# A spectral mixer on one Trainium2 core: a fixed instruction order in the front, paired evacuations, and half of the later filter loads issued from GpSimd

## The chip, the cores and the metric

The kernel runs on one core of one Trainium2 chip. The metric is the device time of one execution in microseconds (us), and smaller is better. The core has five engines that run side by side: TensorE (matmuls), VectorE, ScalarE, GpSimd, and SyncE, which here does nothing but issue transfers. In profile lines they are PE, DVE, ACT, POOL and SP, and a trailing q (as in SPq) marks the sequencer that issues a transfer. Sixteen DMA engines move the data between memory and the core.

Every number below is of fast runs of one core, unless the text says otherwise. A profile is one of the executions. Its span, from the first to the last traced instruction, is 1.5 to 2.1 us shorter than the time of the same execution.

## The reference, cut to what matters

```python
def _A_ref(x, w_r, w_i):                 # x: 1 x 2048 x 512, w: 2048 x 257, all bf16
    X = rfft2(x.astype(float32), axes=(-2, -1))
    X = X * (w_r + 1j * w_i)             # the "filter" W
    return irfft2(X, s=(2048, 512), axes=(-2, -1)).astype(bfloat16)

x  = A_x
h  = x + _A_ref(layernorm(x), A_w_r, A_w_i)
h2 = h + _B_ref(layernorm(h), B_w1, B_b1, B_w2, B_b2)   # token MLP with GELU: not touched here
```

The Fourier transforms are done as matrix products. The change touches only the start, up to the product with the filter.

## The kernel before

The program makes a list of operations and a scheduler orders them on each engine. The operations that matter here come in this order.

1. X comes in as 16 tiles of 128x512, and a constant matrix FP in four pieces. Per tile, the statistics of the layer norm are taken, ScalarE makes the reciprocal deviation `rs`, and FS = FP * rs is made on one of three engines.
2. The first transform (f1) multiplies FS with X. ScalarE copies the result out of PSUM to Y, in halves of 512 columns:

```python
for q in range(8):
    for b in range(2):
        unit = PsumUnit("f1", 1)
        ...                                   # 8 matmuls for tiles 2q and 2q+1
        if (q, b) in Y_DVE:                   # three of the sixteen
            dve(f"y_{q}_{b}", lambda eng, bank, ...: eng.tensor_copy(dst, src(bank)), ...)
        else:
            act(f"y_{q}_{b}", dst, src, ACT.Copy, 512, unit=unit, prio=28)
```

3. The second transform (f2) needs all tiles of Y. Behind it VectorE multiplies with the filter, eight products V, of which the first and the last are cut in halves, so ten operations:

```python
def tt(eng, bank, ...):
    return eng.tensor_tensor(vout, s, win, ALU.mult)       # V = ps * W
K.op(f"v_{u}_{h}", "dve", tt, ins=[wt], outs=[vout], ..., after=wload[u])
```

The filter is read in 28 pieces, in three groups, for products 0, 1 to 3, and 4 to 7. A product waits for all pieces of its group:

```python
for ch, (u0, u1) in enumerate(((0, 1), (1, 4), (4, 8))):
    g0, ng = 4 * u0, 4 * (u1 - u0)
    lst = []
    for w, dram in ((0, A_w_r), (1, A_w_i)):               # real, imaginary
        for comp in range(2):
            d = W[comp::4, g0:g0 + ng, w, :]
            lst.append(dma(f"ld_wp{ch}_{w}{comp}", d,
                bass.AP(dram.tensor, g0 * LW, [[64 * LW, 32], [LW, ng], [1, LW]]),   # rows of 514 bytes
                32 * ng * 514, prio=42 - ch, group=f"w{ch}", rate=300.0))
            ...                                            # the mirrored piece, and two rows for group 0
    for u in range(u0, u1):
        wload[u] = lst
```

Before these pieces SyncE issues X in six pieces, two pieces of FP and the matrices E and MR. The other two pieces of FP are issued by ScalarE.

Of the kernel before, what the change touches and what calls it, by code (L numbers as in the profile page):

```python
# [6 lines left out]
ACT = mybir.ActivationFunctionType  # L7
ALU = mybir.AluOpType
LN_EPS = 1e-5
# [81 lines left out]
def build_consts():  # L91
    c = {}
    n1 = np.arange(NP)
    fp = np.zeros((NP, NS2, NG, 2, 2), np.float64)
    inv = np.zeros((NP, NS2, NP), np.float64)
    for n2 in range(NS2):
        sidx = 16 * n1 + n2
        for g in range(NG):
            gp = _gpos(g)
            for s in range(2):  # L100
                k1 = _slot_k1(g, s)
                c0 = g * 4 + s
                if k1 == 0:
                    fp[:, n2, gp, 0, s] = 1.0
                    fp[:, n2, gp, 1, s] = (-1.0) ** n1
                    inv[c0, n2, :] = 1.0 / S_LEN
                    inv[c0 + 2, n2, :] = ((-1.0) ** n1) / S_LEN
                else:
                    a = TWO_PI * ((k1 * sidx) % S_LEN) / S_LEN
                    fp[:, n2, gp, 0, s] = np.cos(a)  # L110
                    fp[:, n2, gp, 1, s] = -np.sin(a)
                    inv[c0, n2, :] = 2.0 * np.cos(a) / S_LEN
                    inv[c0 + 2, n2, :] = -2.0 * np.sin(a) / S_LEN
    fp = fp.reshape(NP, NS2, NP)
    fp = np.stack([-fp, fp], axis=2)
    for q in range(4):
        c[f"FP{q}"] = fp[:, 4 * q:4 * q + 4]
    c["IF"] = inv
    e = np.zeros((NP, 2, 2, 2, NP), np.float64)
    d2 = np.zeros((NP, 2, 2, 256), np.float64)  # L120
    j = np.arange(NP)
    for par in range(2):
        l = 2 * j + 1 + par
        for dblk in range(2):
            d = dblk * NP + np.arange(NP)
            a = TWO_PI * ((d[:, None] * l[None, :]) % D_LEN) / D_LEN
            e[:, dblk, par, 0, :] = np.cos(a)
            e[:, dblk, par, 1, :] = -np.sin(a)
        d = np.arange(256)
        a = TWO_PI * ((l[:, None] * d[None, :]) % D_LEN) / D_LEN  # L130
        d2[:, par, 0, :] = np.cos(a) / D_LEN
        d2[:, par, 1, :] = np.sin(a) / D_LEN
    e[:, :, 1, 1, 127] = 0.0
    d2[127, 1, 0, :] *= 0.5
    d2[127, 1, 1, :] = 0.0
    m = np.zeros((NP, 2, 2, NP), np.float64)
    for i in range(2):
        mm = _fwd_matrices(i == 1)
        m[0:64, i] = mm
        m[64:128, i] = mm  # L140
    r = np.stack([_inv_matrices(False), _inv_matrices(True)], axis=1)
    c["E"] = e.reshape(NP, 1024)
    c["MR"] = np.concatenate([m.reshape(NP, 512), r.reshape(NP, 512)], axis=1)
    c["D2"] = d2.reshape(NP, 1024)
    return c
# [33 lines left out]
class Builder:  # L179
    def __init__(self, nc, limits):  # L180
        self.nc = nc
        self.ops = []
        self.writer = {}
        self.readers = {}
        self.tensors = {}
        self.limits = limits
        self.cell_cache = {}

# [37 lines left out]
    def op(self, name, engine, emit, ins=(), outs=(), occ=100.0, lat=None, unit=None, pr=False, pw=False,  # L226
           first=False, last=False, prio=0, nbytes=0, is_dma=False, not_before=0.0, after=(), group=None, rate=DMA_RATE):
# [13 lines left out]
        o.rate = rate  # L241
        deps = {id(d): d for d in after}
# [38 lines left out]
    def schedule(self):  # L281
# [13 lines left out]
        order = []  # L295
        while len(order) < len(ops):
            best = None
            for o in ready:
                bank, avail = None, 0.0
# [22 lines left out]
            ready.remove(o)  # L322
            o.sched, o.start = True, st
# [11 lines left out]
            if o.is_dma:  # L335
                x0 = max(st + (3200.0 if st < 4000.0 else 1700.0), dma_free)
                dma_free = x0 + o.bytes / o.rate
                o.finish = dma_free + 200.0
            else:
                o.finish = st + o.lat  # L340
# [143 lines left out]
STAT_ACT = (1, 3)  # L484
RS_GROUPS = ((0,), (2,), (4,), (5,), (6, 7), (8, 9), (10, 11), (12,), (13,), (14,), (15,))
FS_ENG = {4: "act", 7: "act", 9: "dve", 11: "dve", 13: "dve", 14: "act", 15: "dve"}
Y_DVE = ((5, 1), (6, 1), (7, 1))
# [7 lines left out]
def build_kernel(nc, A_x, A_w_r, A_w_i, B_w1, B_b1, B_w2, B_b2, out):  # L495
# [5 lines left out]
    K = Builder(nc, {"f1": 6, "f2": 2, "x": 2, "g1": 2, "g2": 2, "g3": 2, "mm1": 5, "mm1b": 6, "mm2": 8})  # L501
# [13 lines left out]
    def dma(name, dst, src, nbytes, stream="sp", outs=(), ins=(), prio=0, strided=False, after=(), group=None, rate=DMA_RATE,  # L515
            not_before=0.0):
        def emit(eng, bank):
            if strided:
                with nc.allow_non_contiguous_dma(reason="small bias gather"):
# [3 lines left out]
                    rate=rate, occ=1000.0 if stream == "pool" else 640.0 if rate < DMA_RATE else 460.0, not_before=not_before)  # L523
# [40 lines left out]
    def ldf(q, pr_, stream="sp", nb=0.0):  # L564
        sl = slice(4 * q, 4 * q + 4)
        dma(f"ld_FP{q}", FP[:, sl, :, :], cin[f"FP{q}"][:, :, :, :], 1 << 18, outs=[FP[:, sl, :, :]], prio=pr_, stream=stream, not_before=nb)

    for q, (a, b) in enumerate(((0, 2), (2, 4), (4, 6), (6, 8), (8, 12))):
        ldx(a, b, 90 - q)
    ldf(2, 84)  # L570
    ldx(12, 16, 83)
    ldf(3, 82)
    ldf(0, 90, "act")
    act("table", T["tb"][:, 0:1], EPS[:, 0:1], ACT.Abs_reciprocal_sqrt, 1, ins=[EPS[:, 0:1]], prio=88)
    ldf(1, 87, "act", 1800.0)
# [3 lines left out]
    for ch, (u0, u1) in enumerate(((0, 1), (1, 4), (4, 8))):  # L579
        g0, ng = 4 * u0, 4 * (u1 - u0)  # L580
        lst = []
        for w, dram in ((0, A_w_r), (1, A_w_i)):
            for comp in range(2):
                d = W[comp::4, g0:g0 + ng, w, :]
                lst.append(dma(f"ld_wp{ch}_{w}{comp}", d, bass.AP(dram.tensor, g0 * LW, [[64 * LW, 32], [LW, ng], [1, LW]]),
                               32 * ng * 514, prio=42 - ch, group=f"w{ch}", rate=300.0))
# [3 lines left out]
                               32 * nh * 514, prio=42 - ch, group=f"w{ch}", rate=300.0))  # L590
                if g0 == 0:
                    d = W[2 + comp::4, 0, w, :]
                    lst.append(dma(f"ld_wz{ch}_{w}{comp}", d, bass.AP(dram.tensor, 32 * LW, [[64 * LW, 32], [1, LW]]),
                                   32 * 514, prio=42 - ch, group=f"w{ch}", rate=300.0))
# [21 lines left out]
    ZT, BV = T["ZT"], T["bv"]  # L616
    K.op("zt", "dve", lambda eng, bank: eng.memset(ZT[:, :], 0.0), outs=[ZT[:, :]], occ=200.0, prio=60)  # L617
# [9 lines left out]
    def fs_op(i):  # L627
        e = FS_ENG.get(i, "pool")
        rs = RS[:, i:i + 1]
        if e == "act":  # L630
            act(f"fs{i}", FS[:, i, :, :], FP[:, i, :, :], ACT.Copy, 256, ins=[FP[:, i, :, :]], scale=rs, prio=30)
        else:
            dve(f"fs{i}", lambda eng, bank: eng.tensor_scalar(FS[:, i, :, :], FP[:, i, :, :], rs, None, op0=ALU.mult),  # L633
                [FP[:, i, :, :], rs], [FS[:, i, :, :]], 120, prio=30, engine=e, lat=920.0 if e == "pool" else None)

    def stat_act(i):
# [3 lines left out]
        nm = NM[:, i:i + 1]  # L640
        dve(f"nm_{i}", lambda eng, bank: eng.tensor_scalar(nm, SM[:, i:i + 1], -1.0 / D_LEN, None, op0=ALU.mult), [SM[:, i:i + 1]], [nm], 1, prio=33, engine="pool", lat=210.0)
        dve(f"bv_{i}", lambda eng, bank: eng.tensor_scalar(BV[:, i:i + 1], nm, nm, LN_EPS, op0=ALU.mult, op1=ALU.subtract), [nm], [BV[:, i:i + 1]], 1, prio=33, engine="pool", lat=210.0)
        act(f"rs_{i}", RS[:, i:i + 1], V1[:, i:i + 1], ACT.Abs_reciprocal_sqrt, 1, ins=[V1[:, i:i + 1]], bias=BV[:, i:i + 1],
            scale=-1.0 / D_LEN, prio=32)
        fs_op(i)

    def stat_dve(grp):
        a, b = grp[0], grp[-1] + 1
        for i in grp:
# [3 lines left out]
            dve(f"st_{i}", lambda eng, bank, i=i, x=x: eng.bn_stats(ST[:, i, 0:6], x), [x], [ST[:, i, 0:6]], 512, prio=25)  # L653
# [15 lines left out]
    Yv = Y[:].rearrange("p b y g (n k) -> p b (y g) n k", k=4)  # L669
    for q in range(8):  # L670
        for b in range(2):
            unit = PsumUnit("f1", 1)
            lastmm = {}
            for n in range(2):
                n2 = 2 * q + n
                lo = X[:, n2, b * NP:b * NP + NP]
                hi = X[:, n2, 256 + b * NP:256 + b * NP + NP]
                f = FS[:, n2, 1, :]
                f2 = bass.AP(f.tensor, f.offset, [list(f.ap[0]), [0, 2], [1, NP]])
                fm = FS[:, n2, :, :]  # L680

                def o(bank, n=n):
                    return ps[:, bank, n * 256:n * 256 + 256]
                mm(f"f1_{n2}_{b}a", o, lo, f2, unit, True, False, n == 0, 14, 256, ins=[lo, f])
                lastmm[n] = mm(f"f1_{n2}_{b}b", o, hi, fm, unit, False, True, False, 14, 256)

            def src(bank):
                v = ps[:, bank, :].rearrange("p (n g k) -> p n g k", n=2, k=4)
                return v.rearrange("p n g k -> p g n k")
            dst = Yv[:, b, :, 2 * q:2 * q + 2, :]  # L690
            if (q, b) in Y_DVE:
                dve(f"y_{q}_{b}", lambda eng, bank, dst=dst, src=src: eng.tensor_copy(dst, src(bank)), [], [dst], 512, unit=unit, prio=28)
            else:
                act(f"y_{q}_{b}", dst, src, ACT.Copy, 512, unit=unit, prio=28)
            for n in range(2):
                for w_ in range(WARM_AFTER[2 * q + n] if b == 1 else 0):
                    warm(f"warmf{q}{n}{w_}", wu, 13, after=[lastmm[n]], last=2 * q + n == LAST_WARM)
# [183 lines left out]
```

## Time and profile before

| | before |
|---|---|
| time, median of the first 3 runs (lowest to highest) | 134.06 us (133.94 to 134.62) |
| span of the profile, mean granted TensorE clock | 132.4 us, 1.000 |
| front, to the end of ScalarE's last Y (VectorE's last ends at 18.93) | 18.57 us |
| first V operation starts; last one ends | 21.48; 39.36 us |
| filter group 1 / 2 / 3 complete in the trace | 15.37 / 22.90 / 30.11 us |

The first view is part 4 of the page of before, the chain of work that ended last, by engine and line with its share of the span. TensorE holds half of it, and the V products are the next largest entry.

```profile
PE ps L531 50%; DVE V L739 13%; DVE H L799 7%; ACT Y L549 5%; DVE TT L790 4%; DVE TT L792 4%; DVE HH L804 4%; DMA X<-in_A_x_dram 3%; POOL FS L633 1%; ACT rs L549 1%; ACT FS L549 1%; ACT JK L549 1%; DVE OUT L829 1%; ACT PQ L549 0%; PE ps L62
```

The next is the timeline of VectorE in before: start, duration, engine, source line, operation, output and inputs, count, and in brackets how long the engine was idle just before and what ended that idleness. The ten V operations run in one block from 21.48 us without a wait worth showing. After them VectorE waits for TensorE, and from 42.63 us it is the busy engine.

```profile
21.48 17.88 DVE L739 TENSOR_TENSOR V<-ps,W 128x1024 bf16<-128x1024 f32 x10 [0.94 <-PE ps L531]
42.63 0.42 DVE L790 TENSOR_TENSOR TT<-ps,X 128x256 f32<-128x256 f32 x1 [3.27 <-PE ps L531]
```

The timeline of SyncE's sequencer in before shows when the filter pieces are issued: group 1 from 5.80 us (twelve pieces), group 2 from 13.66 us, group 3 from 18.97 us (eight pieces each). Each issue takes about 0.65 us.

```profile
5.80 3.95 SPq L521 DMA_DIRECT2D W<-in_A_w_r_dram  x6
...
13.66 2.60 SPq L521 DMA_DIRECT2D W<-in_A_w_r_dram  x4
16.30 2.62 SPq L521 DMA_DIRECT2D W<-in_A_w_i_dram  x4
18.97 3.33 SPq L521 DMA_DIRECT2D W<-in_A_w_r_dram  x4
```

The last line comes from the timeline of ScalarE in before. Two 512-column evacuations take 1.06 us from the first's start to the second's end; one starts every 0.48 us.

```profile
9.93 1.06 ACT L549 ACTIVATE Y<-ps 128x512 bf16<-128x512 f32 x2
```

### The profile page before, as it was taken

The page shows a single profiled execution, that of the slowest core. Times are in us where ns is not written, and L with a number is a line of the kernel's source. Part 1 is how long each engine was busy: PE and PEld are TensorE (multiplying, and loading weights), DVE is VectorE, ACT ScalarE, POOL GpSimd, SP SyncE. Part 2 cuts the span into 40 slices and gives each one's busy share as a digit, 9 for nine tenths or more (in the row PEclk, how much of TensorE's full clock was granted, in tenths as well). Part 3 has the DMA queues.
Part 4 walks back from the last instruction along what each step waited for, and adds up shares of the span by engine and source line. Part 5 has one row for each costly group of instructions (what it writes and reads, how often), then busy time and mean ns, then how long its engine had stood idle before and what let it go on. Part 6 is the DMA issues. An engine that isn't in the chain of part 4 may idle for free.

```text
span 132.4 us, 2013 instructions
## 1 busy us (share of the span) xinstructions
PE 123.7 (93%) x776; PEld 74.5 (56%) x786; DVE 69.3 (52%) x127; ACT 63.3 (48%) x146; POOL 12.4 (9%) x33
## 2 busy tenths in 40 slices
PE   6989989999977979999999999999999999999990
PEld 2436656788666736544434444456666666666660
DVE  0499867999981999999960000000242332423322
ACT  4579976978966999986689322222000000000000
POOL 0199920000300000000000000000000000000000
PEclk9999999999999999999999999999999999999999
DMA  2999699999999999992000000000111112111121
GB/s 80 375 396 364 153 244 273 286 322 283 419 426 417 410 408 411 417 295 74 0 0 0 0 0 0 5 0 0 40 40 70 49 40 82 42 57 62 40 79 40
DMA packets 16648, 22.16 MB, mean 167 GB/s; under 512 B 2720, under 2 KB 12960, under 8 KB 16128
## 3 DMA queue, kind: packets, MB, share of 16 engines
q1 hardware_dynamic: 16352, 21.52, 47.5%
q10 hardware_dynamic: 288, 0.52, 1.1%
q8 instruction: 6, 0.10, 0.3%
q14 instruction: 2, 0.02, 0.0%
HBM read 19.95 MB, written 2.10 MB: 167 GB/s over the span
## 4 chain that ended last, share of the span: by engine, by line
PE 51%; DVE 32%; ACT 9%; DMA 3%; POOL 2%; issue 1%; DVEq 0%; ACTq 0%
PE ps L531 50%; DVE V L739 13%; DVE H L799 7%; ACT Y L549 5%; DVE TT L790 4%; DVE TT L792 4%; DVE HH L804 4%; DMA X<-in_A_x_dram 3%; POOL FS L633 1%; ACT rs L549 1%; ACT FS L549 1%; ACT JK L549 1%; DVE OUT L829 1%; ACT PQ L549 0%; PE ps L621 0%
## 5 line engine op out<-in xcount | busy, mean ns | idle before, releaser
L531 PE MATMUL ps<-HH,W 128*128 128x512 bf16 (+1 forms) x173 | 40.3, 379 | 1.3 <-DVE HH L804 0.9
L531 PE MATMUL ps<-GT,W 128*128 128x512 bf16 (+1 forms) x172 | 37.9, 379 | 0.2
L829 DVE SCALAR_TENSOR_TENSOR OUT<-ps,B2f,H 128x512 bf16<-128x512 f32 x16 | 12.0, 750 | 48.7 <-PE ps L531 48.7
L531 PEld LDWEIGHTS ps<-GT,W 128*128 128x128 bf16 (+1 forms) x176 | 25.3, 144 | 12.8
L531 PEld LDWEIGHTS ps<-HH,W 128*128 128x128 bf16 (+1 forms) x176 | 17.2, 100 | 21.2 <-DVE HH L804 1.9
L739 DVE TENSOR_TENSOR V<-ps,W 128x2048 bf16<-128x2048 f32 (+1 forms) x10 | 17.9, 1856 | 0.9 <-PE ps L531 0.9
L549 ACT ACTIVATE GT<-ps,B1f 128x512 bf16<-128x512 f32 (+1 forms) x11 | 7.1, 689 | 14.6 <-PE ps L531 14.6
L549 ACT ACTIVATE JK<-H,nm 128x512 bf16<-128x512 bf16 x16 | 11.6, 722 | 3.0 <-DVE H L799 2.9
L653 DVE BATCH_NORM_STATS2 st<-X 128x6 f32<-128x512 bf16 x14 | 9.2, 669 | 4.1 <-DMA X<-in_A_x_dram 4.1
L621 PE MATMUL ps<-ZT 128*128 128x512 bf16 x32 | 9.6, 434 | 1.6 <-DVE ZT L617 1.2
L799 DVE TENSOR_TENSOR H<-ps,TT 128x512 bf16<-128x512 f32 x16 | 10.9, 682 | 0.0
L549 ACT ACTIVATE PQ<-ps 128x512 bf16<-128x512 f32 x16 | 8.9, 602 | 3.5 <-PE ps L531 3.3
L531 PE MATMUL ps<-EM,PQ 128*128 128x256 bf16 x64 | 9.0, 273 | 0.8 <-ACT PQ L549 0.7
L531 PE MATMUL ps<-EM,V 128*128 128x128 bf16 x128 | 9.2, 219 | 0.5 <-DVE V L739 0.5
L549 ACT ACTIVATE EO<-ps 128x512 bf16<-128x512 f32 x16 | 9.2, 596 | 0.9 <-PE ps L531 0.9
L549 ACT ACTIVATE CS<-ps 128x512 bf16<-128x512 f32 x15 | 8.3, 607 | 2.1 <-PE ps L531 2.1
L531 PE MATMUL ps<-EM,Y 128*128 128x256 bf16 x64 | 8.7, 273 | 0.4 <-ACT Y L549 0.4
L531 PE MATMUL ps<-FS,X 128*128 128x256 bf16 x64 | 8.4, 274 | 0.5 <-POOL FS L633 0.4
L531 PEld LDWEIGHTS ps<-EM,V 128*128 128x128 bf16 x128 | 7.5, 98 | 2.3 <-issue 1.4
L633 POOL TENSOR_SCALAR FS<-FP,rs 128x256 bf16<-128x256 bf16 x9 | 8.6, 965 | 0.6 <-ACT rs L549 0.5
L790 DVE TENSOR_TENSOR TT<-ps,X 128x256 f32<-128x256 f32 x16 | 6.7, 417 | 3.3 <-PE ps L531 3.3
L531 PEld LDWEIGHTS ps<-EM,PQ 128*128 128x128 bf16 x64 | 6.2, 98 | 2.9 <-ACT PQ L549 0.9
(36 smaller groups left out, 79.1 us busy)
## 6 DMA issues: line engine op xcount, KB each, us to landing
W<-in_B_w_dram SPq DMA_DIRECT2D x4, 1376.0 KB, 11.7
W<-in_B_w_dram SPq DMA_DIRECT2D x10, 512.0 KB, 18.3
out_dram<-OUT SPq DMA_DIRECT2D x16, 128.0 KB, 1.7
W<-in_A_w_r_dram SPq DMA_DIRECT2D x4, 257.0 KB, 4.5
W<-in_A_w_i_dram SPq DMA_DIRECT2D x4, 257.0 KB, 5.0
X<-in_A_x_dram SPq DMA_DIRECT2D x4, 256.0 KB, 5.0
X<-in_A_x_dram SPq DMA_DIRECT2D x2, 512.0 KB, 6.6
W<-in_A_w_r_dram SPq DMA_DIRECT2D x4, 192.8 KB, 3.3
```

Source lines behind the costliest of these rows:

```text
L531: return K.op(name, "pe", lambda eng, bank: eng.matmul(outf(bank), lhsT, rhs, start=start, stop=stop), ins=ins or [lhsT, rhs], occ=occ, la ...
L549: return eng.activation(dst, s, func, **kw)
L621: return K.op(name, "pe", lambda eng, bank: eng.matmul(ps[:, bank, :], ZT[:, 0:NP], ZT[:, :], start=True, stop=True), ins=[ZT[:, :]], occ= ...
L633: dve(f"fs{i}", lambda eng, bank: eng.tensor_scalar(FS[:, i, :, :], FP[:, i, :, :], rs, None, op0=ALU.mult), [FP[:, i, :, :], rs], [FS[:, ...
L653: dve(f"st_{i}", lambda eng, bank, i=i, x=x: eng.bn_stats(ST[:, i, 0:6], x), [x], [ST[:, i, 0:6]], 512, prio=25)
L739: return eng.tensor_tensor(vout, s, win, ALU.mult)
L790: dve(f"tl_{s2}", lambda eng, bank, tt=tt, xl=xl: eng.tensor_tensor(tt[:, 0, :], ps[:, bank, 256:512], xl, ALU.add), [xl], [tt[:, 0, :]], ...
L792: dve(f"th_{s2}", lambda eng, bank, tt=tt, xh=xh: eng.tensor_tensor(tt[:, 1, :], xh, ps[:, bank, 256:512], ALU.subtract), [xh], [tt[:, 1, ...
L799: return eng.tensor_tensor(hs.rearrange("p (h d) -> p h d", h=2), e, tt[:, :, :], ALU.add)
L804: dve(f"hh_{s2}", lambda eng, bank, s2=s2, hs=hs: eng.tensor_scalar(HH[:, s2, :], hs, NM[:, s2:s2 + 1], R2[:, s2:s2 + 1], op0=ALU.add, op1 ...
L829: dve(f"fin{s2}", lambda eng, bank, dst=dst, bia=bia, hs=hs: eng.scalar_tensor_tensor(dst, ps[:, bank, :], bia, hs, op0=ALU.add, op1=ALU.add),
```

## The change

As I read the diff, the intent is a shorter front. Lists fix the order of the front's instructions on VectorE, ScalarE, GpSimd and TensorE. Fourteen 512-column evacuations became seven of 1024 columns. X is loaded in smaller first pieces, and all of X and FP from SyncE. To make up for SyncE's longer list, the eight imaginary pieces of filter groups 2 and 3 are issued by GpSimd. The diff, cut to its core:

```diff
-STAT_ACT = (1, 3)
-RS_GROUPS = ((0,), (2,), (4,), (5,), (6, 7), (8, 9), (10, 11), (12,), (13,), (14,), (15,))
-FS_ENG = {4: "act", 7: "act", 9: "dve", 11: "dve", 13: "dve", 14: "act", 15: "dve"}
-Y_DVE = ((5, 1), (6, 1), (7, 1))
+STAT_ACT = (5,)
+RS_GROUPS = ((0,), (1, 2), (3,), (4,), (6, 7), (8, 9), (10, 11), (12, 13), (14, 15))
+FS_ENG = {0: 'dve', 2: 'act', 4: 'act', 9: 'act', 11: 'act', 12: 'dve', 13: 'dve', 14: 'dve', 15: 'dve'}
+Y_EVAC = (('pair', 'act'), ... six more ..., ('single', ('dve', 'act'), ('dve', 'dve')))
+FRONT = {
+    "dve": """bn_0 ag_0 bn_1 ag_1 bn_2 ag_2 bn_3 bn_4 ag_3 fs_0 ag_4 bn_6 bn_7 ag_6 bn_8 ag_7 bn_9 ag_8 bn_10 ...""",
+    "act": """rs_0 s1_5 rs_1 s2_5 rs_3 fs_2 rs_4 rs_5 fs_4 yp_0 rs_6 yp_1 yp_2 rs_8 rs_10 fs_9 fs_11 yp_3 ...""",
+    "pool": """bv_5 fs_1 fs_3 fs_5 fs_7 fs_6 fs_8 fs_10""",
+    "pe": """f1_0 f1_1 f1_2 f1_4 f1_3 f1_5 f1_7 f1_6 f1_9 f1_8 f1_11 f1_10 f1_12 f1_13 f1_15 f1_14""",
+}
 ... (the scheduler takes these orders as forced; its model of a DMA's delay is changed)
-    for q, (a, b) in enumerate(((0, 2), (2, 4), (4, 6), (6, 8), (8, 12))):
-        ldx(a, b, 90 - q)
-    ldf(2, 84)
-    ldx(12, 16, 83)
-    ldf(3, 82)
-    ldf(0, 90, "act")
-    ldf(1, 87, "act", 1800.0)
+    for q, (a, b) in enumerate(((0, 1), (1, 2), (2, 4), (4, 6))):
+        ldx(a, b, 99 - q)
+    ldf(0, 95, stall=700.0)
+    ldx(6, 8, 94)
+    ldf(1, 93)
+    ldx(8, 10, 92)
+    ldx(10, 12, 91)
+    ldf(2, 90)
+    ldx(12, 16, 89)
+    ldf(3, 88)
 ...
         for w, dram in ((0, A_w_r), (1, A_w_i)):
+            wq = {"stream": "pool", "not_before": 13000.0} if ch and w else {}
+            gr = f"w{ch}p" if ch and w else f"w{ch}"
 ... (each filter dma: group=gr, **wq)
-                act(f"y_{q}_{b}", dst, src, ACT.Copy, 512, unit=unit, prio=28)
+            y_op(f"yp_{q}", kind[1], 2 * q, 4, 0, f1u[2 * q, 0], True)      # 1024 columns, two PSUM banks
```

## The prediction

> **What bounds the kernel now.** The chain of waits has stages: front 0 to 18.6 us (statistics of X, scaling FP into FS, first transform, evacuation to Y), a VectorE stage of ten V products (21.5 to 39.3 us, back to back), a VectorE-bound stage 42.6 to 68 us, then TensorE alone to 129 us. The change touches the front and the transfers that feed V. V, the later VectorE work and the matmuls keep their counts, so at best a shorter front shifts everything behind it.
>
> The front is bound by ScalarE. In the timeline it starts at 4.89 us, when X lands, and from 9.15 to 18.57 us it is never idle: 13 evacuations (cadence 0.48 us), small rs operations (0.18), FS pieces (0.41). VectorE is also full from 6.1 to 15.8 us (14 statistics at 0.66 each); GpSimd runs nine FS at 0.93. TensorE idles and runs 12 fillers.
>
> **What changes, with costs.**
> 1. The first X piece is halved and FP leaves the ScalarE queue. In the DMA packets the first 512 KB (X and FP interleaved) were in by 4.15 us and X released at 4.87. With 128 KB alone first, release about 3.5 us: first statistics 1.3 us earlier. The rest of X is nearly unchanged; FP's first piece lands about 6.1 to 6.8.
> 2. ScalarE loses two statistics passes, 1.2 us, and three small operations; gains one FS, 0.41. VectorE gains one statistic and one FS, loses 512 columns of evacuation.
> 3. Pairing: fourteen 512-wide evacuations become seven 1024-wide ones. At 0.833 ns per column a 512 costs 0.427 of its 0.48 cadence, so a pair should cost about 0.91: saving 0.06 each, 0.4 in all. (The Trainium skill, "ScalarE: Activation LUTs", What ACT_TABLE_LOAD costs, gives that rate and an overlap of successive ACTIVATEs of about 93 ns; the trace agrees.) Pairing is a small gain.
> 4. Walking the new order by hand with those durations: first pair starts about 8.2 us; seven pairs, five rs, two FS and a half tile give 8.4 us; small waits for GpSimd's FS. Last Y about 16.9 (range 16.4 to 17.6) against 18.57.
> 5. Filter: 28 pieces were issued by SP, 0.65 each, to 25.7 us; they landed in three groups at 15.0, 21.7 and 29.6 us. The V product needing the third started only about 30.4. Now SP starts them 1.7 us later, but eight go out from GpSimd after its last FS, from about 13.5 us. While they flow the DMA engines already show shares near 1.0 at about 280 GB/s (514 B packets), and the skill ("DMA: Bandwidth & Descriptors", Issuing engines are not separate DMA queues) says other issuers only save issue time. So I expect issue relief, third group about 28.5 to 29.5, and a shifted V stage waiting up to 0.5 us in total for W.
>
> **On the critical path:** 1.7 us of front, minus about 0.3 of filter waits: 1.4 us. Predicted 132.6 us, range 131.4 to 133.6; faster by over 2% 0.13, within 2% 0.83, slower 0.04.
>
> **What would show it.** First statistics near 3.5 us; 1024-wide Y ACTIVATE near 1.0 us long; last Y near 16.9; V starting near 19.8; V idle before W under 0.6 us; everything after V shifted by the same amount, stage lengths unchanged within 0.3.
>
> **What would make it wrong.** GpSimd needing over 2 us per issue (no such transfer in this trace) delays V by microseconds; pairs slower across two PSUM banks; FP's first piece late, holding f1; filter bandwidth worse with two queues. Better than 131.4 needs V to start before 18.8.

## More of the kernel before

The DMA view of before lists, per kind of transfer, the size of one and the median time from its issue to its landing. These are the pieces of group 2, real part and imaginary part.

```profile
W<-in_A_w_r_dram SPq DMA_DIRECT2D x4, 192.8 KB, 3.3
W<-in_A_w_i_dram SPq DMA_DIRECT2D x4, 192.8 KB, 3.9
```

The completion times of filter groups 1 / 2 / 3 (15.37 / 22.90 / 30.11 us) are those of the last completion report of each group in the trace; no view prints them.

## The result, and the profile after

The changed kernel takes 139.71 us (median of 4 fast runs, 139.44 to 139.85) against 134.00 us for the kernel before in the same rounds. The ratio is 1.0416, with a 95% interval of 1.0378 to 1.0454: it is slower by about 4%. A ratio here is the mean time of one kernel's fast runs over that of the other's fast runs of the same rounds, so it is not quite the ratio of the medians quoted. The prediction was 132.6 us, in a range of 131.4 to 133.6. It was wrong in direction and outside its range. Of the 5.7 us between the medians the profiled span shows 5.0; the rest lies outside the traced instructions (see the last section).

| | before | after |
|---|---|---|
| span, mean clock | 132.4 us, 1.000 | 137.4 us, 0.988 |
| first statistics | 4.89 | 2.89 |
| last Y of ScalarE / of VectorE ends | 18.57 / 18.93 | 18.22 / 18.27 |
| first V starts | 21.48 | 21.11 |
| last V ends | 39.36 | 44.57 |
| filter groups 1 / 2 / 3 complete | 15.37 / 22.90 / 30.11 | 18.23 / 28.30 / 31.83 |

This is part 4 of the page of after. Issuing by SyncE and the landing of the real filter pieces have appeared on the chain that ended last, with 11% and 8% of the span.

```profile
PE ps L551 53%; SPq L541 11%; DMA W<-in_A_w_r_dram 8%; DVE H L858 7%; DVE TT L849 4%; DVE TT L851 4%; DVE HH L863 4%; ACT PQ L569 2%; DVE V L798 2%; ACT CS L569 1%; DVE OUT L888 1%; PE ps L646 0%
```

In the timeline of VectorE in after, the V block is broken. Two operations run at 21.11 us, and then VectorE waits 4.86 us for the real filter pieces. Two more gaps of 0.19 and 0.34 us follow, for TensorE.

```profile
21.11 2.35 DVE L798 TENSOR_TENSOR V<-ps,W 128x1024 bf16<-128x1024 f32 x2 [0.93 <-PE ps L551]
28.33 6.68 DVE L798 TENSOR_TENSOR V<-ps,W 128x2048 bf16<-128x2048 f32 x3 [4.86 <-DMA W<-in_A_w_r_dram]
35.20 4.49 DVE L798 TENSOR_TENSOR V<-ps,W 128x2048 bf16<-128x2048 f32 x2 [0.19 <-PE ps L551]
40.02 4.55 DVE L798 TENSOR_TENSOR V<-ps,W 128x2048 bf16<-128x2048 f32 x3 [0.34 <-PE ps L551]
47.92 0.42 DVE L849 TENSOR_TENSOR TT<-ps,X 128x256 f32<-128x256 f32 x1 [3.35 <-PE ps L551]
```

These gaps are the loss. They add up to 4.86 + 0.19 + 0.34 = 5.39 us; the V block started 0.37 us earlier and its own operations took 0.2 us more, so its end moved by about 5.2 us. The first operation of the next stage moved from 42.63 to 47.92 us, by 5.29 us. The block of matmuls that starts at 64.86 us before starts at 70.14 us after, by 5.28 us. Behind V the stages kept their length; only over the rest, to the end of the span, were 0.3 us won back (the span grew by 5.0 us).

SyncE's timeline in after shows its filter issues starting at 7.58 us, 1.78 us later than before. SyncE has four transfers more in front of them, at 0.43 to 0.48 us each. The last line below has the eight real pieces of groups 2 and 3, of which the first four are group 2.

```profile
7.58 4.10 SPq L541 DMA_DIRECT2D W<-in_A_w_r_dram  x6
11.72 3.83 SPq L541 DMA_DIRECT2D W<-in_A_w_i_dram  x6
15.59 10.86 SPq L541 DMA_DIRECT2D W<-in_A_w_r_dram  x8
```

GpSimd's timeline in after has its eight issues from 14.72 us, 0.65 us each. The prediction feared 2 us each; that did not happen.

```profile
14.72 5.23 POOL L541 DMA_DIRECT2D W<-in_A_w_i_dram  x8
```

The DMA view of after shows the pieces of group 2, in the same columns as for before. The imaginary pieces from GpSimd need 4.0 us. The real ones from SyncE need 7.2 us, where they had needed 3.3. Of the 64 completion reports of these four real pieces (16 each), 63 had come by 27.03 us and the last came at 28.30, so 1.27 us of the wait are one late share of one piece.

```profile
W<-in_A_w_i_dram POOLq DMA_DIRECT2D x4, 192.8 KB, 4.0
W<-in_A_w_r_dram SPq DMA_DIRECT2D x4, 192.8 KB, 7.2
```

Part of the reason can be read in the packet records of after. The next two lines count them between 22 and 25 us, per queue: number of packets, megabytes, share of the 16 engines' time. Queue q0 is GpSimd's and q1 is SyncE's.

```profile
q0 software_dynamic: 229, 0.76, 85.3%
q1 hardware_dynamic: 234, 0.11, 17.2%
```

The two queues had about the same number of packets, 229 and 234. But a packet of GpSimd's queue carried eight filter rows (4112 bytes in most records), and one of SyncE's queue a single row of 514 bytes. So GpSimd's queue moved 0.76 MB and SyncE's 0.11 MB. The sum of the view, 296 KB per us, is close to that of before with SyncE alone. The view of before for a stretch of the same length, 22.9 to 25.9 us, shows 0.85 MB in 3 us, or 283 KB per us.

```profile
q1 hardware_dynamic: 1704, 0.85, 107.9%
```

When GpSimd's queue had nearly run dry (12 packets in this stretch), SyncE's had the engines almost to itself again. This is SyncE's queue between 25.5 and 28 us in after: 0.69 MB in 2.5 us.

```profile
q1 hardware_dynamic: 1380, 0.69, 114.7%
```

The turns were not equal all the time. This is the same view of after for 18 to 22 us, while the pieces of group 2 from both queues were on their way:

```profile
q0 software_dynamic: 209, 0.66, 56.4%
q1 hardware_dynamic: 1036, 0.52, 47.0%
```

Here SyncE's queue had five times the packets of GpSimd's, and GpSimd's larger packets still moved more than half of the bytes. So equal turns hold for one stretch of this trace and not for the other; why they differ was not settled.

The Trainium skill states the rule in "DMA: Bandwidth & Descriptors", section Queues, rings and completion order: each DMA engine "round-robins between the queue rows it has work for, at *packet* granularity". Equal packet counts are what that says while both queues have work on every engine. This trace agrees from 22 to 25 us (229 and 234); from 18 to 22 us (209 and 1036) it doesn't show such turns. In the prediction I had leaned on another section of the same page, Issuing engines are not separate DMA queues, which says that issuing from more engines only saves issue time. For the sum that held. For the order of arrival it did not: from 22 to 25 us the pieces that were wanted last (GpSimd's group 3) had most of the bytes (0.76 MB), while pieces that were wanted first (the rest of SyncE's group 2) were still under way.

The front gained almost nothing either. The first statistics start at 2.89 us, earlier than predicted, but the later pieces of X land later: the timeline of VectorE in after has statistics waiting for tile 8 until 9.75 us, and in the fixed order the aggregate of tile 7 waits behind it.

```profile
2.89 0.70 DVE L680 BATCH_NORM_STATS2 st<-X 128x6 f32<-128x512 bf16 x1 [1.78 <-DMA X<-in_A_x_dram]
...
9.75 0.69 DVE L680 BATCH_NORM_STATS2 st<-X 128x6 f32<-128x512 bf16 x1 [0.79 <-DMA X<-in_A_x_dram]
```

The view by windows gives, for the stretch from 6 to 7 us, busy times of PE, weight loads, VectorE, ScalarE and GpSimd, then the granted clock, the DMA share and GB/s. First before, then after: the DMA engines had a dip that they did not have before.

```profile
6.00:7.00 1.00, 1.00 (x6) 0.29 (x3) 0.87 (x2) 1.00 (x5) 0.79 (x2) 1.00 1.07 418
```

```profile
6.00:7.00 1.00, 1.00 (x6) 0.36 (x4) 1.00 (x2) 1.00 (x4) 0.34 (x2) 1.00 0.75 289
```

The paired evacuations cost what was predicted: 1.02 us long, and two in 1.92 us.

```profile
9.13 1.02 ACT L569 ACTIVATE Y<-ps 128x1024 bf16<-128x1024 f32 x1 [0.31 <-PE ps L551]
...
10.76 1.92 ACT L569 ACTIVATE Y<-ps 128x1024 bf16<-128x1024 f32 x2
```

Last, TensorE waited for V, and its clock fell: the timeline of TensorE in after, and the windows view with the clock in the column after PE's busy time.

```profile
30.76 1.04 PE L551 MATMUL ps<-CS,EM 64*128 64x256 bf16 x8 [4.54 <-DVE V L798]
```

```profile
30.30:33.70 3.40, 2.94 (x26) 0.50 1.01 232
```

The skill's page "TensorE: Matmul & The Clock Gate", Part 1, says that the clock halves after an idle window of about 3.4 us. The trace of after fits that: TensorE was idle for 4.54 us, from 26.22 to 30.76, and the clock was halved from 30.29 for 3.41 us. The trace of e1 below does not: there TensorE was idle for only 2.29 us, from 25.71 to 28.00, and the clock was halved all the same, from 28.77 for 3.41 us. So a shorter gap can be enough. The cost of the half clock in after was not measured on its own; the two gaps of VectorE for TensorE (0.53 us together) begin after it.

### The profile page after: what moved, and what is told of

It is laid out like the page before. It is cut to its first block, busy times and chain, and to the rows that moved or that the text cites. A ratio compares the mean times of both kernels' runs of the same rounds, so it can differ in the third digit from the quotient of the medians.

```text
span 137.4 us, 2012 instructions
## 1 busy us (share of the span) xinstructions
PE 125.6 (91%) x786; PEld 76.8 (56%) x786; DVE 69.7 (51%) x130; ACT 62.5 (45%) x135; POOL 14.5 (11%) x35
## 4 chain that ended last, share of the span: by engine, by line
PE 53%; DVE 21%; SPq 11%; DMA 8%; ACT 4%; issue 1%
PE ps L551 53%; SPq L541 11%; DMA W<-in_A_w_r_dram 8%; DVE H L858 7%; DVE TT L849 4%; DVE TT L851 4%; DVE HH L863 4%; ACT PQ L569 2%; DVE V L798 2%; ACT CS L569 1%; DVE OUT L888 1%; PE ps L646 0%
## 5 line engine op out<-in xcount | busy, mean ns | idle before, releaser
L646 PE MATMUL ps<-ZT 128*128 128x512 bf16 x34 | 11.2, 470 | 1.3 <-DVE ZT L589 1.2
L680 DVE BATCH_NORM_STATS2 st<-X 128x6 f32<-128x512 bf16 x15 | 9.8, 673 | 3.0 <-DMA X<-in_A_x_dram 3.0
L551 PE MATMUL ps<-CS,EM 64*128 64x256 bf16 x64 | 5.2, 289 | 4.9 <-DVE V L798 4.5
L551 PEld LDWEIGHTS ps<-EM,V 128*128 128x128 bf16 x128 | 8.1, 104 | 2.0 <-issue 1.0
```

Of the source, the lines that this page charges most:

```text
L551: return K.op(name, "pe", lambda eng, bank: eng.matmul(outf(bank), lhsT, rhs, start=start, stop=stop), ins=ins or [lhsT, rhs], occ=occ, la ...
L646: return K.op(name, "pe", lambda eng, bank: eng.matmul(ps[:, bank, :], ZT[:, 0:NP], ZT[:, :], start=True, stop=True), ins=[ZT[:, :]], occ= ...
L680: dve(f"bn_{i}", lambda eng, bank, i=i, x=x: eng.bn_stats(ST[:, i, 0:6], x), [x], [ST[:, i, 0:6]], 512, prio=25)
```

## The experiments

The theory (A): the loss is late filter data. Part of it comes from SyncE starting the filter 1.8 us later, and part from GpSimd's packets holding back SyncE's. The first rival: it is only SyncE's later start. The second rival: the new front, its order and pairs, costs time by itself, or GpSimd's transfers are harmful wherever they are. Each run is also compared with the kernel before on the same chip.

### e1: the change, with the whole filter on SyncE

```diff
-            wq = {"stream": "pool", "not_before": 13000.0} if ch and w else {}
-            gr = f"w{ch}p" if ch and w else f"w{ch}"
+            wq = {}
+            gr = f"w{ch}"
```

> The changed kernel with all 28 filter pieces issued by SP again. If GpSimd's transfers are the cause of the loss (theory), the 4.9 us wait of the third V product for W is gone, V runs from 21.1 us with under 0.6 us of waits for W, the granted clock has no half-speed stretch, and the time is 133.2 to 134.2 us. If instead the filter was late because SP begins it 1.7 us later after twelve X and FP issues (rival 1), a wait of over 1.5 us for W remains and the time is over 135.5.

Measured: 136.38 us, ratio 1.0151 (1.0098 to 1.0204). Group 2 was complete at 25.54 us. VectorE's timeline of e1:

```profile
20.60 2.35 DVE L798 TENSOR_TENSOR V<-ps,W 128x1024 bf16<-128x1024 f32 x2 [0.93 <-PE ps L551]
25.57 6.68 DVE L798 TENSOR_TENSOR V<-ps,W 128x2048 bf16<-128x2048 f32 x3 [2.61 <-DMA W<-in_A_w_i_dram]
32.67 8.99 DVE L798 TENSOR_TENSOR V<-ps,W 128x2048 bf16<-128x2048 f32 x5 [0.42 <-PE ps L551]
```

The wait fell from 4.86 to 2.61 us. The time I expected, 133.2 to 134.2, was missed. So GpSimd's queue accounts for the larger part of the loss, but the later start of the filter alone still costs two microseconds. The first rival holds for that part. This run also bears on the clock: three of its four runs had a mean clock of 0.985 to 0.987 and spans of 134.4 to 134.7 us, and one had clock 1.000 and a span of 134.7 us. The stretch at half clock cost nothing visible there.

### e2: the kernel before, with the eight imaginary pieces on GpSimd

```diff
+            wq = {"stream": "pool", "not_before": 14500.0} if ch and w else {}
+            gr = f"w{ch}p" if ch and w else f"w{ch}"
 ... (each filter dma: group=gr, **wq)
```

> The kernel before with the eight imaginary pieces of the second and third filter groups issued by GpSimd after its last FS (about 16.0 us), front untouched. Theory (GpSimd's packets of 4112 bytes win the turn-taking of the DMA engines against SP's 514-byte packets, so what SP issues later is held up until GpSimd's ring is empty, and only an urgent piece behind it costs time): the real pieces of the second group are issued by 16.3 and are mostly through before GpSimd's data begin near 17.5, so they land by about 21 and the third V product waits under 1 us; time 133.7 to 135. Rival 2 (GpSimd-issued transfers are slow or disturb the chip whatever the order): several us lost as in the changed kernel, 137 to 140.

Measured: 135.16 us, ratio 1.0066 (1.0012 to 1.0119), just above the 133.7 to 135 that I expected. The second rival would have needed 137 to 140. VectorE's timeline of e2, and the packets between 22 and 25 us:

```profile
21.35 2.36 DVE L741 TENSOR_TENSOR V<-ps,W 128x1024 bf16<-128x1024 f32 x2 [0.93 <-PE ps L531]
24.84 15.56 DVE L741 TENSOR_TENSOR V<-ps,W 128x2048 bf16<-128x2048 f32 x8 [1.13 <-issue]
```

```profile
q0 software_dynamic: 236, 0.76, 85.5%
q1 hardware_dynamic: 275, 0.14, 21.0%
```

The packet counts are again close (236 and 275), with 0.76 and 0.14 MB. It costs little here because SyncE's real pieces of group 2 had mostly gone before GpSimd's first packet at 18.08 us, and landed at 20.06 us. Group 2 was complete at 24.76 us, and the third V operation started at 24.84. The view put that idleness down to "issue", but the landing 0.08 us earlier says what ended it. So GpSimd as an issuer need not cost several microseconds: it matters when its bytes come in relation to pieces that are wanted sooner.

### e3: the change, with GpSimd's third group held back until SyncE's second has landed

```diff
+            if ch == 1 and w == 0:
+                gate = lst
+            if ch == 2 and w:
+                wq["after"] = gate[:4]
```

> The changed kernel, but GpSimd's four pieces of the third group wait until SP's four of the second have landed; same pieces on the same issuers, only their order in time changed. Theory: without the third group in front of them the second group's real pieces land about 3 to 4 us earlier than 28.3, near 24 to 25; the V wait falls from 4.9 to about 1 to 2 us, time 135 to 137. If the order does not matter (rival 2), the wait stays above 4 us and the time near 139.7 or more.

Measured: 137.95 us (median of five runs, one of them slow), ratio 1.0278 (1.0212 to 1.0344) from the four fast ones. The profile fell in the slow run (span 137.9 us, against 135.4 to 136.6 in the fast ones), so only the order of events is taken from it; the sizes of its waits are not those of a fast run. VectorE's timeline of e3:

```profile
25.11 6.68 DVE L802 TENSOR_TENSOR V<-ps,W 128x2048 bf16<-128x2048 f32 x3 [1.69 <-DMA W<-in_A_w_r_dram]
36.07 8.95 DVE L802 TENSOR_TENSOR V<-ps,W 128x2048 bf16<-128x2048 f32 x5 [4.27 <-DMA W<-in_A_w_i_dram]
```

Group 2 came at 25.09 us where it had come at 28.30. That fits the held-back pieces having delayed it, and the fast runs lie below those of the change (1.0278 against 1.0416), but no fast trace shows it. GpSimd then issued its third group only at 25.37 us, and group 3 became the late one: the gate moved the wait. The expected 135 to 137 us was missed, probably for that reason.

### e4: the change, with group 2 all on GpSimd and group 3 all on SyncE

```diff
-            wq = {"stream": "pool", "not_before": 13000.0} if ch and w else {}
-            gr = f"w{ch}p" if ch and w else f"w{ch}"
+            wq = {"stream": "pool", "not_before": 13000.0} if ch == 1 else {}
+            gr = f"w{ch}p" if ch == 1 else f"w{ch}"
```

> The changed kernel, but GpSimd issues all eight pieces of the second group (needed first) and SP all eight of the third. Theory: the favoured ring now carries what V needs first; the second group lands by about 23, V waits under 1 us for it, the third group is held up but lands by about 29.5; time 133.2 to 134.8, although the same number of pieces comes from GpSimd. Rival 2 (GpSimd's transfers slow in themselves): the second group lands at 26 or later, the time is over 137.

Measured: 137.36 us, ratio 1.0221 (1.0167 to 1.0274). Group 2 landed at 26.98 us, where I had expected about 23. VectorE's timeline of e4, and the packets between 18 and 21 us:

```profile
27.01 15.54 DVE L798 TENSOR_TENSOR V<-ps,W 128x2048 bf16<-128x2048 f32 x8 [3.49 <-DMA W<-in_A_w_i_dram]
```

```profile
q1 hardware_dynamic: 713, 0.36, 51.0%
q0 software_dynamic: 132, 0.40, 46.1%
```

This is a miss that limits the theory. GpSimd's queue is not simply first. In these 3 us it had 132 packets and SyncE's 713, so the turns were not equal, and SyncE's less urgent pieces moved nearly as many bytes (0.36 against 0.40 MB). A queue without waiting packets on an engine could give up its turn there, but that was not settled: by 20 us GpSimd had issued all eight pieces and 161 of their 384 packets of 4112 bytes had been served, so its queue as a whole was not empty, and from 20 to 21 us it had 32 of them served against 320 packets of SyncE's. e4 came out on the side of the second rival (group 2 at 26 us or later, time over 137). e2 speaks against that rival in its general form, since there the same number of pieces from GpSimd cost 0.7%. What remains is that pieces from GpSimd cost more when they compete with SyncE's pieces, and that these runs don't tell by which rule.

### e5: the new front with the loads of before, filter on SyncE

```diff
 ... (e1's edit, and:)
-    for q, (a, b) in enumerate(((0, 1), (1, 2), (2, 4), (4, 6))):
-        ldx(a, b, 99 - q)
-    ldf(0, 95, stall=700.0)
 ... (the rest of the new loads)
+    for q, (a, b) in enumerate(((0, 2), (2, 4), (4, 6), (6, 8), (8, 12))):
+        ldx(a, b, 99 - q)
+    ldf(2, 90)
+    ldx(12, 16, 89)
+    ldf(3, 88)
+    ldf(0, 97, "act")
+    ldf(1, 95, "act", 1800.0)
```

> The changed front (fixed orders, pairs, one statistics tile on ScalarE), but X, FP and the filter loaded as in the kernel before: two FP pieces from ScalarE's queue, wider X pieces, all filter pieces from SP. Theory A (SP's filter issues start 1.9 us later because of the load change, and the second group has only 0.8 us of slack): the first filter issue is back at 5.8 us, the second group lands near 22.9, V starts near 20.6 to 21, waits for W at most 1.2 us; time 133.0 to 134.2, 1.5 to 2.5 below the run with only the filter back on SP. Rival: the new front itself moves something later that costs, then V still waits over 2 us or the time stays over 135.5.

Measured: 134.07 us, ratio 1.0009 (0.9980 to 1.0038). VectorE's timeline of e5 has the whole V block in one piece again:

```profile
21.25 17.88 DVE L795 TENSOR_TENSOR V<-ps,W 128x1024 bf16<-128x1024 f32 x10 [0.94 <-PE ps L551]
```

The fixed order and the pairs are neutral by themselves. With the loads of before, V starts 0.23 us earlier than before (I had expected 20.6 to 21) and waits for nothing.

### e6: the kernel before with the change's loads of X and FP

```diff
-    for q, (a, b) in enumerate(((0, 2), (2, 4), (4, 6), (6, 8), (8, 12))):
 ... (and the five lines after it)
+    for q, (a, b) in enumerate(((0, 1), (1, 2), (2, 4), (4, 6))):
+        ldx(a, b, 99 - q)
+    ldf(0, 95)
+    ldx(6, 8, 94)
 ... (as in the change)
```

> The kernel before with only the X and FP loads of the change (twelve pieces, all from SP), filter on SP, order of the engines as its own scheduler gives it. Theory A: the first filter issue moves from 5.8 to about 7.7, the second group lands at 25 to 25.7, the third V product waits 1 to 3 us for W; time 135 to 136.5. If the later filter start does not matter, no wait for W above 0.5 us and time under 134.5.

Measured: 136.30 us, ratio 1.0183 (1.0144 to 1.0222). Filter issues start at 7.65 us, group 2 is complete at 24.95 us, and group 3 at 32.61 us. VectorE's timeline of e6:

```profile
24.97 6.69 DVE L742 TENSOR_TENSOR V<-ps,W 128x2048 bf16<-128x2048 f32 x3 [1.26 <-PE ps L531]
32.63 8.95 DVE L742 TENSOR_TENSOR V<-ps,W 128x2048 bf16<-128x2048 f32 x5 [0.97 <-DMA W<-in_A_w_i_dram]
```

The loads alone bring a loss, by the two waits of 1.26 and 0.97 us. The first of them is put down to TensorE, but group 2 was complete at 24.95 us, 0.02 us before the wait ended, and a product can't start before that. So the landing sets the start.

### e7: a combination meant to keep both gains

New front, first X pieces halved, FP's first two pieces back on ScalarE's queue, the whole filter on SyncE, the matrix MR issued by GpSimd, 17 filler matmuls instead of 20 at the start, and tile 7's aggregate moved ahead of tile 8's statistics:

```diff
-bn_7 ag_6 bn_8 ag_7 bn_9 ag_8
+bn_7 ag_6 ag_7 bn_8 bn_9 ag_8
-N_WARM = 20
+N_WARM = 17
 ... (loads as in e5 with (0, 1), (1, 2), (2, 4) first; ld_MR with stream="pool")
```

> A version meant to beat both: new front, filter on SP, first two X pieces single tiles, first two FP pieces from ScalarE's queue after its table load, MR issued by GpSimd after its FS pieces (one issue less ahead of the filter), 17 fillers instead of 20, and the aggregate of tile 7 moved before the statistics of tile 8 on VectorE. Expected: filter issues from about 6.0 us, second group at about 22.5 to 23, last Y at 17 to 17.6, V from about 20, a W wait of 0.5 to 1.5 us; time 132.3 to 133.8.

Measured: 134.33 us, ratio 1.0026 (1.0001 to 1.0052). The expectation of 132.3 to 133.8 was missed. V started at 21.27 us, and it waited 0.24 us for group 3. Earlier first tiles did not shorten the front.

### e8: e1 with the filter cut into groups of other sizes

If the supply of W is the whole loss of e1, then moving the cuts, with the same bytes and the same number of pieces, should remove it.

```diff
-    for ch, (u0, u1) in enumerate(((0, 1), (1, 4), (4, 8))):
+    for ch, (u0, u1) in enumerate(((0, 2), (2, 5), (5, 8))):
```

> The changed kernel with all filter pieces on SP and the three groups cut at 2, 5 and 8 products instead of 1, 4 and 8: same 28 pieces, same bytes, but the twelve first pieces carry 1.05 MB instead of 0.53, so SP's issue time is not wasted on small ones, and each later group is needed later. Theory (supply of W binds the V stage; its slack was used up by the load change): second group wanted at about 25.1 us and landing near 25, third wanted at about 31.8 and landing near 31; V starts at 20.6 and waits for W under 0.5 us in all; time 132.7 to 133.7, below both kernels. If the bandwidth of the filter itself is the limit and not the issue, waits of 1.5 us or more remain and the time is 135 or more.

Measured: 133.90 us, ratio 0.9991 (0.9960 to 1.0022), where e1 had 1.0151. VectorE's timeline of e8:

```profile
21.80 17.80 DVE L798 TENSOR_TENSOR V<-ps,W 128x1024 bf16<-128x1024 f32 x10 [0.94 <-PE ps L551]
```

The groups were complete at 19.59, 25.64 and 31.00 us, each before it was wanted, and the block is whole. The time is just above the 132.7 to 133.7 that I expected. This shows that the loss of e1 was the wait for W. In this profile V also started 1.2 us later than in e1 (21.80 against 20.60), which gave W more time; e10 below, which starts at 20.84, keeps a wait of 0.18 us.

### e9: the kernel before with the same cut

> Control: the kernel before with the same new cut of the groups. There V already runs without a wait for W, so the cut should change nothing: 133.6 to 134.4 us, ratio within 0.4% of 1, the filter complete about 1 us earlier than 30.1.

Measured: 133.84 us, ratio 0.9985 (0.9961 to 1.0008), the same edit as e8 on the kernel before. There was no wait to remove, and nothing was gained. So the cut is no gain in itself; it repairs.

### e10: e8, with two repairs in the front

Tile 7's aggregate ahead of tile 8's statistics, and 18 filler matmuls instead of 20 (the diff is e8's and the first four lines of e7's, with 18).

> As e8, with the aggregate of tile 7 moved before the statistics of tile 8 on VectorE and 18 fillers instead of 20. Expected 0 to 0.4 us below e8: the stall behind tile 8 was 0.1 to 0.8 us, but ScalarE is busy without a break from 8.9 us on.

Measured: 133.66 us, ratio 0.9975 (0.9952 to 0.9998). It is the best version found, and it is still within 2% of before. V starts at 20.84 us, and one wait of 0.18 us for W remains. This is the earliest V start but one of all the runs, and it is worth a third of a microsecond.

### e11: the change as it is, with the new cut alone

The diff is e8's single line, and GpSimd keeps its pieces.

> The changed kernel as it is, GpSimd issuing the imaginary pieces of the second and third group, with only the new cut of the groups. Theory: SP's real pieces of the second group still stand behind GpSimd's third-group pieces on every DMA engine, land at 27 to 29, V waits 2 to 4 us for them; time 136 to 138.5. If the slack of the groups was all that was missing, V waits under 0.6 us and the time is 132.7 to 133.8.

Measured: 135.77 us, ratio 1.0130 (1.0102 to 1.0157). VectorE's timeline of e11:

```profile
21.27 4.55 DVE L798 TENSOR_TENSOR V<-ps,W 128x1024 bf16<-128x1024 f32 x3 [0.93 <-PE ps L551]
27.43 13.34 DVE L798 TENSOR_TENSOR V<-ps,W 128x2048 bf16<-128x2048 f32 x7 [1.61 <-PE ps L551]
```

Group 2's real pieces, from SyncE, landed at 27.41 us, and its imaginary pieces, from GpSimd, at 21.69 us. The V operation that needs them started at 27.43. With the new cut GpSimd still costs 1.6 us of wait. That is less than the 2 to 4 us expected, and the time is below the expected 136 to 138.5. (The view puts the wait down to TensorE; the real pieces landed 0.02 us before it ended.)

### e12: e10 with FP's first piece on ScalarE's queue

This asks why X lands later with the new loads: whether FP in the same queue is what holds it up.

```diff
-    ldf(0, 95, stall=700.0)
+    ldf(0, 95, stream="act", nb=150.0)
```

> As e10, with the first FP piece issued from ScalarE's queue after its table load instead of from SP. Open question: why X and FP arrive 1 us or more later with the changed loads; in all profiles with them the DMA engines are busy only 66 to 88% in the us from 6 to 7, just when the first FP piece flows. If FP in the same ring is the stall, the share from 6 to 7 us is back above 93%, tile 8 of X lands at 9.0 us or earlier (9.5 in e10), V starts near 20.2 to 20.5 and the time is 0.3 to 0.6 us below e10, near 133.2. If the gap has another cause (the single-tile X pieces), it stays, and the time is that of e10 within 0.3 us.

Measured: 134.22 us, ratio 1.0036 (1.0005 to 1.0068). The dip in the DMA share between 6 and 7 us stayed (0.79; 0.71 in e10, 0.77 in e1, 1.07 before), and tiles 4 and 5 landed at 7.16 us. So the place of FP's first piece alone is not the cause. The time, which was to be that of e10 within 0.3 us if the dip stayed, was about 0.6% above it. I overlooked that e7 narrows the question: it too has single-tile first pieces of X, but FP's first two pieces on ScalarE's queue, and its DMA share from 6 to 7 us was 1.06, without a dip. So the single-tile pieces by themselves don't make the dip. The cause stays open.

### The runs together

| | filter issued by SyncE alone | half of groups 2 and 3 by GpSimd |
|---|---|---|
| kernel before, old cut | 1 | 1.0066 (e2) |
| kernel before, new cut | 0.9985 (e9) | |
| new front, loads of before | 1.0009 (e5) | |
| kernel before, new loads | 1.0183 (e6) | |
| new front and new loads, old cut | 1.0151 (e1) | 1.0416 (the change) |
| new front and new loads, new cut | 0.9991 (e8), 0.9975 (e10) | 1.0130 (e11) |

The parts do not add up. Adding GpSimd costs 0.7% in the kernel before, and about 1.0416 / 1.0151 = 1.026, so 2.6%, with the new front and new loads. My reading is that the reason is the time at which they meet: in e2 GpSimd's first issue came at 15.93 us, when SyncE had issued nearly all real pieces of group 2 (13.66 to 16.26); in the changed kernel it came at 14.72 us, before SyncE's first (15.59). No run moves this time alone.

## Why the prediction was wrong, point by point

- **"a shifted V stage waiting up to 0.5 us in total for W": wrong, and it decided the result.** The waits for W were 4.86 us. I had followed only group 3, and put its landing at 28.5 to 29.5 us; it landed at 31.83, but V waited for group 2. Group 2 had 0.86 us of slack in before, and I never set its landing beside its use. I had also read that landing too early: 21.7 us, where the trace has 22.90. SyncE's later start used up that slack and more: with the whole filter on SyncE the wait is 2.61 us (e1). Issuing half of groups 2 and 3 from GpSimd added the rest.
- **"other issuers only save issue time ... So I expect issue relief": right for the sum, wrong for the order.** The sum was no lower than before (296 against 283 KB per us). What I missed is who gets it: GpSimd's packets were up to eight times as large, and with about equal packet counts it moved 0.76 against SyncE's 0.11 MB in 3 us. The page that I quoted has the rule of turns by packet in another section. e2 shows similar counts; the stretch from 18 to 22 us and e4 do not, so it is shown that issuing from GpSimd delays SyncE's pieces (28.30 us in the change, 25.54 in e1), and it is not shown by which rule the engines divide their time.
- **"The rest of X is nearly unchanged": wrong.** Tiles 12 to 15 landed at 12.39 us instead of 10.79, and tiles 6 and 7 at 7.57 instead of 7.39. With them the predicted front gain of 1.7 us (last Y at 16.9) shrank to 0.35 us (ScalarE's last Y at 18.22). The fixed order made it worse in one place, where tile 7's aggregate stood behind tile 8's statistics. With the loads of before the new front gained only 0.2 us of V start (e5), so the hand-walked 1.7 us was also too large by itself.
- **Pairs "about 0.91": right.** Two pairs took 1.92 us, a length of 1.02 and a cadence of 0.90 us. The Trainium skill, "ScalarE: Activation LUTs", What ACT_TABLE_LOAD costs, gives 186 ns + 0.833 ns per column, which is 1.04 us for 1024 columns; the trace agrees. Where two pairs follow each other the overlap was 0.10 and 0.12 us, against the 93 ns that the prediction quoted.
- **First statistics "near 3.5 us": right in direction**, 2.89 us measured. It was worth nothing, because the later tiles set the pace.
- **"Everything after V shifted by the same amount": right**, by 5.28 us in the other direction.
- **"filter bandwidth worse with two queues" was named as a danger.** It was close, but not the thing: the sum was no lower, and its division between the queues changed. "GpSimd needing over 2 us per issue" did not happen (0.65 us).
- **Left open:** why X and FP land later with the new loads; the cost of the half-clock stretch in the changed kernel; why GpSimd's queue got so few turns in e4, and from 18 to 22 us in the changed kernel.

## What to carry to other kernels

Before transfers are moved or reordered, write down for each consumer when its data lands and when it is wanted: the V stage here had no visible wait and only 0.2 to 0.9 us of slack, so a faster front or a later supply soon turns into a wait. When two queues feed the same DMA engines, look at the packet sizes and not only at the sum: here a later-needed transfer with packets of 4112 bytes had 0.76 MB in a stretch in which a sooner-needed one with packets of 514 bytes had 0.11 MB. When a stage waits for groups of pieces, the sizes of the groups are a cheap thing to move: one changed line took e1's loss away.

## What the Trainium skill lacked or had wrong

- "DMA: Bandwidth & Descriptors", Issuing engines are not separate DMA queues: it says that issuing on several engines only saves issue time. The sum agreed (296 against 283 KB per us), but the section doesn't say which transfers gain and which are delayed. SyncE's group 2 pieces went from 3.3 to 7.2 us from issue to landing.
- Same page, Queues, rings and completion order: turns by packet agreed from 22 to 25 us (229 and 234 packets), and not from 18 to 22 us (209 and 1036) or in e4 (132 and 713). It gives about 9 to 17 descriptors per packet as typical. The records here show one 514-byte row per packet for SyncE, and eight rows (4112 bytes) for GpSimd.
- "TensorE: Matmul & The Clock Gate", Part 1: an idle window of about 3.4 us before the clock halves fits after (4.54 us idle) and not e1, where 2.29 us of idle time were followed by 3.41 us of half clock.
- No page that I read says how long an issue itself can stall: the last of SyncE's real filter pieces took 5.18 us to issue in the changed kernel (median 0.63), in the stretch in which both queues were busy, and SyncE's next transfer was issued only at 26.49 us.
- No page that I read says that the time outside the traced span depends on a kernel's transfers. It was 1.5 to 1.6 us with the loads of before, about 1.8 with the new loads, and 1.8 to 2.05 with GpSimd's transfers. So 0.3 to 0.5 us of the loss is not in the trace at all, and e10, whose mean span is about 0.6 us below that of before, keeps only about 0.35 us of it in its mean time.
